# Second-layer matmuls of a unit in one run instead of small groups between first-layer products

## The chip, the cores and the metric

The kernel runs on one core of a Trainium2 chip. The time is in device microseconds (us) of one execution; three executions of the kernel before took 1178.77, 1180.59 and 1181.42 us, a median of 1180.59 us.

## The reference

Three stages follow each other. Attention over 2 x 576 tokens, 8 heads of 64, with a bias from a small network of the relative position. Then a mixture of 8 experts over the 1152 tokens, each a ReLU network 512 -> 1024 -> 512, whose outputs are weighted by a matrix P (from gate logits, normalised 8 times by rows and columns) and added. Last a network 512 -> 2048 -> 512 with ELU. All is float32.

```python
for e in range(E):                      # 8 experts
    h = np.maximum(x @ w1[e], 0.0)      # first layer
    ye = h @ w2[e]                      # second layer
    out += P[:, e:e + 1] * ye
...
h = x @ w_in                            # 512 -> 2048
g = np.where(h > 0.0, h, alpha * (np.exp(np.minimum(h, 0.0)) - 1.0))
return (g @ w_out).astype(np.float32)
```

## The kernel before

**Tiling.** The two networks are cut into 20 *halves* `he` of 512 hidden values: 0 to 15 are the halves of the 8 experts, 16 to 19 the ELU network. The tokens are two groups `n`: group 0 has 512 tokens (four tiles of 128), group 1 has 640 (five tiles). One *step* is (he, n); steps run in the order (0,0), (0,1), (1,0) and so on. The change touches 30 of the 40 steps.

**First layer.** A step has two *units* `u` of 256 hidden values. A unit is a 2 x 2 block product done with seven products in place of eight; sums of weight blocks and token blocks are prepared before. Float32 precision comes from splitting each operand into a high and a low part, so a product is 6 matmuls on TensorE (`m`, line 539): two halves of the contraction by three pairs (high-high, high-low, low-high). They are 256 columns wide in group 0 and 320 in group 1. The seven products of a unit use three PSUM banks: 1, 4, 6 and 7 add up in `b1`, 3 and 5 in `b2`, 2 is alone in `b3`. After a product ScalarE copies the bank out (`fork`, line 552, tiles `p1`, `p5`, `u2`, `u3`) or VectorE adds two parts (`add`, line 571, tiles `c1`, `c22`). A later product may add to a bank only when the copy of the earlier state is done: 6 waits for `p1`, 7 for `u2`, 3 for `p5`, and 4 for `u3`, the copy after 7. Product 4 of a unit is therefore done inside the next unit (`prev`). Then `hidden` applies ReLU or ELU and splits the result into high `hh` (ScalarE, line 602) and low `hl` (VectorE, line 605).

**Second layer.** The tokens' tiles of step (he, n) are multiplied by the second weights in the *next* step: `l2` yields 12 matmuls (`y`, line 727, 512 columns) for each token tile, four hidden blocks f by three pairs. So a step after group 0 has 48 of them and one after group 1 has 60. Tiles 0 and 1 are done together (f 0 and 1 of both, then f 2, then f 3), so that tile 0 ends with matmul 21 and tile 1 with matmul 24; the tiles behind them go one by one. In the ELU halves three tiles go together and the third has a bank of its own. Else a tile takes one of two PSUM banks (`psB`). When a tile is done, VectorE adds it to the accumulator (`l2_evac`, line 758, `acc<-y,P,acc`), and only then can the next tile but one use the bank.

**What sets the order.** `mm` gives every matmul of the two networks a rank, so TensorE's order is the order in which the code yields them: `step` runs through the products of `l1` and after product number i lets `ys`, the second-layer matmuls, advance to a share of their count:

```python
adv(lead + round((ny - lead) * max(0, i + 1 - o) / (m - o - finish)))
```

With 14 products and 48 or 60 `ys`, 3 to 5 second-layer matmuls stand behind every product. VectorE, ScalarE, GpSimd and the DMA queue of SyncE are filled by a list scheduler (`Plan.order`) with costs written into the code; each engine then runs its own list in order. `hooks` start the splitting of the next weights (`split1`) after a given product. Beside this work VectorE converts the last network's weights from float64 (`conv`, tiles `cw`, `ca`, `cb`).

Of the kernel before, what the change touches and what calls it, by code (L numbers as in the profile page):

```python
# [18 lines left out]
E = 8  # L19
# [67 lines left out]
class Plan:  # L87
# [3 lines left out]
    def buf(self, tag, bufs, alloc, tile=None):  # L91
        b = Buf(tag, alloc, tile)
        q = self.tags.setdefault(tag, [])
        b.prev = q[-bufs] if len(q) >= bufs else None
        b.before = q[-1] if q else None
        if b.prev is not None:
            b.prev.closed = True
        b.closed = False
        q.append(b)
        return b  # L100

    def op(self, eng, fn, r=(), w=(), after=(), ready=0.0, rank=None):
        o = Op()
        o.eng = eng if isinstance(eng, list) else [eng]
        o.fn, o.ready, o.idx, o.rank = fn, ready, len(self.ops), rank
        deps = set(after)
        for k in list(r) + list(w):
            b = k[0]
            assert not b.closed, b.tag
            if k in w:  # L110
                if b.prev is not None:
                    deps.update(b.prev.users)
                if b.before is not None:
                    deps.update(b.before.first)
                if not b.users or not b.first_done:
                    b.first.append(o)
            else:
                b.first_done = True
            b.users.append(o)
        for k in r:  # L120
            rd, wr = self.last.setdefault(k, ([], []))
            deps.update(wr)
        for k in w:
            rd, wr = self.last.setdefault(k, ([], []))
            deps.update(rd)
            deps.update(wr)
        for k in w:
            self.last[k] = ([], [o])
        for k in r:
            if k not in w:  # L130
                self.last[k][0].append(o)
        deps.discard(o)
        o.deps = deps
        self.ops.append(o)
        return o
# [85 lines left out]
def attention_moe_elu_ffn_kernel(  # L221
# [77 lines left out]
    def w1_sum(t, st, i, eng):  # L299
        r = t.rearrange("p (o k f) -> p o k f", o=2, k=2)  # L300
        a11, a12, a21, a22 = r[:, 0, :, 0:128], r[:, 1, :, 0:128], r[:, 0, :, 128:256], r[:, 1, :, 128:256]
        x, y, op = [
            (a21, a22, ALU.add), (st[:, 0], a11, ALU.subtract), (a11, a21, ALU.subtract), (a12, st[:, 1], ALU.subtract),
        ][i]
        eng.tensor_tensor(out=st[:, i], in0=x, in1=y, op=op)
# [70 lines left out]
    def cD(n, psum=0):  # L376
        return 0.16 + 0.00105 * n + 0.05 * psum
# [4 lines left out]
    def build():  # L382
# [44 lines left out]
        def hi_lo(b, key, dst, src, srck, n, after=(), alt=False):  # L427
            bh, bl = b

            def hi(e):  # L430
                if e == "A":
                    act.activation(out=dst(bh.get()), in_=src(), func=ACTF.Copy)  # L432
                else:
                    dve.tensor_copy(dst(bh.get()), src())

            op([("A", cA(n))], hi, r=srck, w=[(bh, key)], after=after)
            op(
                [("D", cD(n))],
                lambda e: eng[e].tensor_tensor(  # L439
                    out=dst(bl.get()), in0=src(), in1=dst(bh.get().bitcast(F32)), op=ALU.subtract  # L440
                ),
                r=srck + [(bh, key)],
                w=[(bl, key)],
                after=after,
            )

        def new_st():
            return buf("st", 1, lambda: stp.tile([128, 4, 2, 128], F32, tag="st", name="st"))

        def split1(he, u):  # L450
            if he >= HE or (he, u) in wt:
                return
            t = rawb[1, he, u]
            wt[he, u] = b = [
                buf(f"w1{x}", 2, lambda x=x: wgt.tile([128, 7, 2, 128], F32R, tag=f"w1{x}", name=f"w1{x}")) for x in "hl"
            ]
            st = new_st()
            for i in range(4):
                op(
                    [("D", cD(256))],  # L460
                    lambda e, i=i: w1_sum(t.get(), st.get(), i, eng[e]),
                    r=[(t, 0)] + ([(st, i - 1)] if i in (1, 3) else []) + ([(st, 1)] if i == 3 else []),
                    w=[(st, i)],
                )
            for i in range(4):
                n = 256 if i == 1 else 512
                dst = [slice(0, 2), 2, slice(3, 5), slice(5, 7)][i]
                hi_lo(
                    b, i, lambda x, dst=dst: x[:, dst], lambda i=i: w1_src(t.get(), st.get())[i][1],
                    [(t, 0)] if i < 2 else [(st, 2 * i - 4), (st, 2 * i - 3)], n, alt=he >= 2 * E,  # L470
                )
            load_next()
# [211 lines left out]

        prev = [None]

        def l1(he, n):
            for u in range(2):
                x = None
                for i in (1, 4, 2, 5, 6, 3, 7):  # L690
                    if i == 4:
                        if prev[0] is None:
                            continue
                        product(prev[0], 4)
                        evac(prev[0], 4)
                    else:
                        if x is None:
                            x = unit(he, n, u)
                        product(x, i)
                        evac(x, i)  # L700
                    yield i
                prev[0] = x
# [297 lines left out]
        def step(he, n, ys, ny, lead=0, finish=0, hooks={}, tail=0):  # L1000
            m = 14
            done = 0

            def adv(k):
                nonlocal done
                while done < min(k, ny):
                    next(ys)
                    done += 1

            adv(lead)  # L1010
            for i, _ in enumerate(l1(he, n)):
                o = 0 if lead or he < 2 * E or n else L2_OFF
                adv(lead + round((ny - lead) * max(0, i + 1 - o) / (m - o - finish)))
                for f in hooks.get(i, ()):
                    f()
            adv(ny)
            if not tail:
                for _ in ys:
                    pass
# [6 lines left out]
        for _ in l1(0, 0):  # L1026
            pass
# [8 lines left out]
        for he in range(HE):  # L1036
            for n in range(2):
                if (he, n) in ((0, 0), (2 * E, 1)):
                    continue
                if he == 2 * E and n == 0:  # L1040
                    for t in (0, 2, 1, 3):
                        x2t(t)
                    flush()
                    new_ops(0)
                    ops_build(0, 0)
                    ops_build(0, 1)
                    split1(he, 0)
                    ys = l2(he - 1, 1, order1)
                    step(he, 0, ys, 60 - BD_TAIL, lead=BD_LEAD, finish=BD_FIN, hooks={0: [lambda: split1(he, 1)]}, tail=1)
                    flush()  # L1050
                    for _ in ys:
                        pass
                    for t in (4, 8, 5, 7, 6):
                        x2t(t)
                    new_ops(1)
                    for t in (2, 3, 4):
                        ops_build(1, t)
                    split2(he, 0)
                    split2(he, 1)
                    step(he, 1, l2(he, 0, std[0]), 48, lead=BD_LEAD2, finish=BD_FIN2)  # L1060
                    last = (he, 1)
                    continue
                hooks = {}
                if n == 0:
                    split1(he, 0)
                    hooks[1] = [lambda he=he: split1(he, 1)]
                else:
                    if he:
                        split2(he, 0)
                        split2(he, 1)  # L1070
                od = (order1 if last[0] == 2 * E - 1 else std[1]) if last[1] else (order0 if last[0] == 2 * E - 1 else std[0])
                ys = l2(*last, od)
                fin = BD_FIN0 if (he, n) == (2 * E - 1, 1) else 0
                step(he, n, ys, 60 if last[1] else 48, finish=fin, hooks=hooks)
                last = (he, n)
                if not conved:
                    conved = True
                    conv()
# [547 lines left out]
```

## Time and profile before

| what | value |
|---|---|
| three runs | 1178.77, 1180.59, 1181.42 us |
| span of the profiled execution, first to last instruction | 1178.4 us |
| time of that execution around its span | not told apart; the fastest run is 0.4 us over the span, the median 2.2 |
| TensorE busy | 1150.9 us (98%) |
| VectorE, ScalarE busy | 910.4 us (77%), 630.5 us (54%) |
| granted TensorE clock, mean | 0.992 |

Matmuls overlap: a matmul's record of 0.28 to 0.40 us begins before the one ahead of it has ended, so what a matmul costs is the distance from its start to the next one's, not its duration. TensorE's busy time is thus not a sum of costs, and the start times in the timeline are to be used.

### The profile page before, as it was taken

To read this page: it belongs to the slowest core of one execution; us is meant where nothing else is said; L and a number is where in the kernel's file an instruction comes from. 1 tells how busy PE (TensorE), PEld (TensorE's weight loads), DVE (VectorE), ACT (ScalarE), POOL (GpSimd) and SP (SyncE) were. 2 spreads that over 40 slices of the span, in tenths; PEclk is the share of its full clock that TensorE was granted. 3 is DMA by queue.
4 is the path that set the end of the run, shared out by engine and by line. 5 is a ranking of instruction groups with operands and counts; after the bars stand their busy time and mean duration, and the time that the engine had idled before them with its cause. 6 is when DMAs were issued, how large, how long until landed. Compare 5 with 4: busy or idle time off the path is not lost.

```text
span 1178.4 us, 19626 instructions
## 1 busy us (share of the span) xinstructions
PE 1150.9 (98%) x7432; PEld 1001.2 (85%) x7432; DVE 910.4 (77%) x1936; ACT 630.5 (54%) x1428; POOL 68.0 (6%) x91
## 2 busy tenths in 40 slices
PE   7899999999999999999999999999999998999998
PEld 3467988989888898998988988989889887898987
DVE  7887888845687878878778788787776569888875
ACT  7997677644243344444443444444434347776763
POOL 0102552000000000000000000000000002000000
PEclk8999999999999999999999999999999999999999
DMA  7866631111112233333242333332411101111102
GB/s 212 252 220 213 197 112 49 37 54 55 36 40 96 65 105 91 107 92 105 66 132 68 103 91 107 94 103 70 128 46 54 44 11 51 40 54 37 36 1 81
DMA packets 36286, 104.78 MB, mean 89 GB/s; under 512 B 4065, under 2 KB 4193, under 8 KB 36193
## 3 DMA queue, kind: packets, MB, share of 16 engines
q1 hardware_dynamic: 36192, 103.54, 29.1%
q8 instruction: 58, 0.95, 0.3%
q14 instruction: 36, 0.29, 0.1%
HBM read 81.88 MB, written 21.64 MB: 88 GB/s over the span
## 4 chain that ended last, share of the span: by engine, by line
PE 90%; DVE 3%; ACT 1%; issue 1%; POOL 0%; DVEq 0%; ACTq 0%; POOLq 0%
PE y L727 41%; PE m L539 37%; PE sc L1220 3%; PE av L1302 3%; PE tr L1271 2%; PE bps L1424 1%; PE av L1312 1%; PE av L1299 1%; PE lg L883 0%; PE trl L1283 0%; DVE ol L439 0%; ACT et L1245 0%; PE x2t L977 0%; DVE w2l L439 0%; DVE et L1230 0%
## 5 line engine op out<-in xcount | busy, mean ns | idle before, releaser
L539 PE MATMUL m<-oh,w1h 128*128 128x256 f32 (+1 forms) x1120 | 331.3, 296 | 0.5 <-ACT u L552 0.5
L539 PE MATMUL m<-ol,w1h 128*128 128x256 f32 (+1 forms) x1120 | 330.7, 295 | 0.9 <-DVE ol L439 0.8
L539 PE MATMUL m<-oh,w1l 128*128 128x256 f32 (+1 forms) x1120 | 330.2, 295 | 0.0
L727 PE MATMUL y<-w2h,hh 128*128 128x512 f32 x720 | 284.2, 395 | 3.2 <-ACT hh L646 1.5
L727 PE MATMUL y<-w2l,hh 128*128 128x512 f32 x720 | 283.3, 393 | 0.8 <-DVE w2l L439 0.8
L727 PE MATMUL y<-w2h,hl 128*128 128x512 f32 x720 | 283.8, 394 | 0.0
L539 PEld LDWEIGHTS m<-ol,w1h 128*128 128x128 f32 x1120 | 211.8, 189 | 25.2 <-DVE ol L439 1.1
L539 PEld LDWEIGHTS m<-oh,w1h 128*128 128x128 f32 x1120 | 211.6, 189 | 24.7 <-ACT u L552 1.2
L539 PEld LDWEIGHTS m<-oh,w1l 128*128 128x128 f32 x1120 | 211.7, 189 | 0.1
L727 PEld LDWEIGHTS y<-w2h,hh 128*128 128x128 f32 x720 | 135.2, 188 | 19.0 <-ACT hh L646 2.3
L552 ACT ACTIVATE p<-m 128x256 f32<-128x256 f32 (+1 forms) x160 | 65.8, 411 | 158.6 <-PE m L539 154.5
L727 PEld LDWEIGHTS y<-w2h,hl 128*128 128x128 f32 x720 | 135.2, 188 | 17.6
L727 PEld LDWEIGHTS y<-w2l,hh 128*128 128x128 f32 x720 | 135.3, 188 | 16.3 <-DVE w2l L439 1.4
L552 ACT ACTIVATE u<-m 128x256 f32<-128x256 f32 (+1 forms) x160 | 65.8, 411 | 123.3 <-PE m L539 122.9
L602 ACT ACTIVATE hh<-c 128x512 fp32r<-128x512 f32 (+3 forms) x128 | 72.1, 564 | 104.0 <-DVE c L571 104.0
L758 DVE SCALAR_TENSOR_TENSOR acc<-y,P,acc 128x512 f32<-128x512 f32 x126 | 94.5, 750 | 37.9 <-PE y L727 35.7
L605 DVE SCALAR_TENSOR_TENSOR hl<-c,hh 128x512 fp32r<-128x512 f32 (+3 forms) x128 | 77.5, 606 | 20.3 <-ACT hh L602 18.4
L571 DVE TENSOR_TENSOR c<-m,u 128x256 f32<-128x256 f32 (+1 forms) x80 | 36.6, 457 | 56.7 <-PE m L539 56.1
L1230 DVE CUSTOM_DVE_ANT_0 et<-sc,bt 128x576 f32<-128x576 f32 (+1 forms) x80 | 58.0, 751 | 13.5 <-PE sc L1220 12.2
L1245 ACT ACTIVATE et<-et,nmx 128x576 f32<-128x576 f32 (+1 forms) x80 | 61.6, 775 | 0.2 <-DVE nmx L1230 0.2
L432 ACT ACTIVATE w2h<-raw 128x512 fp32r<-128x512 f32 x80 | 48.6, 626 | 21.5 <-PE y L727 11.8
L439 DVE TENSOR_TENSOR w2l<-raw,w2h 128x512 fp32r<-128x512 f32 x80 | 53.9, 692 | 1.5 <-ACT w2h L432 1.5
(138 smaller groups left out, 1550.0 us busy)
## 6 DMA issues: line engine op xcount, KB each, us to landing
raw<-w1p SPq DMA_DIRECT2D x32, 512.0 KB, 3.7
raw<-w2p SPq DMA_DIRECT2D x32, 512.0 KB, 3.6
scr<-o SPq DMA_DIRECT2D x36, 295.5 KB, 3.0
bt<-scr SPq DMA_DIRECT2D x16, 576.0 KB, 4.4
cw<-w1d SPq DMA_DIRECT2D x16, 512.0 KB, 4.6
wsc<-ca SPq DMA_DIRECT2D x32, 256.0 KB, 4.4
cw<-w2d SPq DMA_DIRECT2D x16, 512.0 KB, 4.4
raw<-wsc SPq DMA_DIRECT2D x16, 512.0 KB, 3.6
```

The costliest lines, as they stand in the source:

```text
L432: act.activation(out=dst(bh.get()), in_=src(), func=ACTF.Copy)
L439: lambda e: eng[e].tensor_tensor(out=dst(bl.get()), in0=src(), in1=dst(bh.get().bitcast(F32)), op=ALU.subtract),
L539: lambda e, w=w, o=o, j=j, k=k: pe.matmul(x["ap"](bank), w.get()[:, ai, j, :], o.get()[:, bi, j, :], start=(k == 0 and i in (1, 2, 5)), st ...
L552: lambda e: act.activation(out=b.get()[:, 0:N], in_=x["ap"](bank), func=ACTF.Copy),
L571: lambda e: eng[e].tensor_tensor(out=blk(b.get()[:, half * N:half * N + N], rev), in0=ap(p), in1=ap(q), op=ALU.add),
L602: op([("A", cA(w))], lambda e: act.activation(out=hh(), in_=ap(), func=ACTF.Relu), r=sk, w=wh, after=gate_)
L605: lambda e: dve.scalar_tensor_tensor(out=bl.get()[:, d], in0=ap(), scalar=0.0, in1=hhf(), op0=ALU.max, op1=ALU.subtract),
L727: lambda e, a=a, w=w, f=f, i=i, y=y, c=c: pe.matmul(y.get(), a.get()[:, c], w.get(), start=(f == 0 and i == 0), stop=(f == 3 and i == 2)),
L758: lambda e: dve.scalar_tensor_tensor(out=a.get(), in0=y.get(), scalar=P[0][:, n, e_:e_ + 1], in1=a.get(), op0=ALU.mult, op1=ALU.add),
L1220: pe.matmul(sc[h][0:r, x, 0:HALF], qs[:, h, qc], w[:, h, kc], start=not last, stop=last)
L1230: dve.tensor_tensor_reduce(out=e.rearrange("p (x j) -> p x j", x=2), in0=sc[0:r, :, 0:HALF], in1=biast[hp, t][0:r, h].rearrange("p (x j) - ...
L1245: act.activation(out=e, in_=e, func=ACTF.Exp, scale=-1.0, bias=nmx[0:r, h:h + 1], accum_out=sm[0:r, h:h + 1])
```

## The change

In the steps of halves 3 to 14 and 17 to 19 (`solid`) the products of a unit come in the order 1 2 4 5 6 3 7 in place of 1 4 2 5 6 3 7. No second-layer matmul stands behind products 1, 2, 4, 5, 3 and 7; behind product 6 of the first unit comes one run of half of them (24 or 30), behind product 6 of the second unit the rest. The hook that splits the next weights moves with product 4 from place 1 to place 2. The other steps are as before. Every instruction's work is unchanged.

```diff
+        def solid(he):
+            return 3 <= he < 2 * E - 1 or he > 2 * E
+
         def l1(he, n):
             for u in range(2):
                 x = None
-                for i in (1, 4, 2, 5, 6, 3, 7):
+                for i in (1, 2, 4, 5, 6, 3, 7) if solid(he) else (1, 4, 2, 5, 6, 3, 7):
...
             adv(lead)
-            for i, _ in enumerate(l1(he, n)):
+            for i, k in enumerate(l1(he, n)):
+                if solid(he) and not lead:
+                    if k == 6:
+                        adv(ny if i > 6 else (ny + 1) // 2)
+                    for f in hooks.get(i, ()):
+                        f()
+                    continue
...
                 if n == 0:
                     split1(he, 0)
-                    hooks[1] = [lambda he=he: split1(he, 1)]
+                    hooks[2 if solid(he) else 1] = [lambda he=he: split1(he, 1)]
```

The first place is on TensorE, in the first unit of step (7, 0), where the first two token tiles of the second layer end and the third begins. Before, with `y_6452` the first tile, `y_6476` the second, `y_6547` the third, and `m` a product of the first layer:

```order
L727 MATMUL y_6452<-w2h_6193,hl1_6461 128x512
L539 MATMUL m_6501<-oh0_2695,w1h_6359 128x256
L539 MATMUL m_6501<-ol0_2696,w1h_6359 128x256
L539 MATMUL m_6501<-oh0_2695,w1l_6368 128x256
L539 MATMUL m_6501<-oh0_2695,w1h_6359 128x256
L539 MATMUL m_6501<-ol0_2696,w1h_6359 128x256
L539 MATMUL m_6501<-oh0_2695,w1l_6368 128x256
L727 MATMUL y_6476<-w2h_6193,hh1_6454 128x512
L727 MATMUL y_6476<-w2l_6204,hh1_6454 128x512
L727 MATMUL y_6476<-w2h_6193,hl1_6461 128x512
L727 MATMUL y_6547<-w2h_5772,hh1_6310 128x512
```

Now at the same place (`y_6469`, `y_6483` and `y_6517` are the three tiles; the line of the matmul is 730 in the changed file):

```order
L730 MATMUL y_6469<-w2h_6162,hl1_6471 128x512
L730 MATMUL y_6483<-w2h_6162,hh1_6458 128x512
L730 MATMUL y_6483<-w2l_6169,hh1_6458 128x512
L730 MATMUL y_6483<-w2h_6162,hl1_6471 128x512
L730 MATMUL y_6517<-w2h_5777,hh1_6302 128x512
```

The product that stood between the end of the first tile and the start of the third has moved away; three matmuls are left between them.

The second place is on VectorE, in the same unit: the additions of these two tiles to the accumulators `acc4` and `acc5`, and what stands ahead and behind. Before:

```order
L439 TENSOR_TENSOR w1l_6480<-raw_6077,w1h_6473 128x256
L834 TENSOR_SCALAR cb_6465<-ca_6348 128x512
L837 SCALAR_TENSOR_TENSOR cb_6465<-cw_6297,cb_6465 128x512
L842 TENSOR_TENSOR ca_6348<-ca_6348,cb_6465 128x512
L758 SCALAR_TENSOR_TENSOR acc4_3516<-y_6452,P_4096,acc4_3516 128x512
L571 TENSOR_TENSOR c1_6495<-m_6501,u2_6528 128x256
L758 SCALAR_TENSOR_TENSOR acc5_3533<-y_6476,P_4096,acc5_3533 128x512
```

Now:

```order
L439 TENSOR_TENSOR w1l_6461<-st_6389,w1h_6450 128x512
L439 TENSOR_TENSOR w1l_6461<-raw_6055,w1h_6450 128x256
L840 SCALAR_TENSOR_TENSOR cb_6370<-cw_6205,cb_6370 128x512
L845 TENSOR_TENSOR ca_6279<-ca_6279,cb_6370 128x512
L761 SCALAR_TENSOR_TENSOR acc4_3516<-y_6469,P_4096,acc4_3516 128x512
L761 SCALAR_TENSOR_TENSOR acc5_3533<-y_6483,P_4096,acc5_3533 128x512
L571 TENSOR_TENSOR c1_6446<-m_6448,u2_6474 128x256
```

The two additions now follow each other; a piece of the weight conversion (`cb`, `ca`) still stands right ahead of them.

## Rows read from the trace of the kernel before

**Rows 1.** The page's chain that ended last, by line.

```profile
PE y L727 41%; PE m L539 37%; PE sc L1220 3%; PE av L1302 3%; PE tr L1271 2%; PE bps L1424 1%; PE av L1312 1%; PE av L1299 1%; PE lg L883 0%; PE trl L1283 0%; DVE ol L439 0%; ACT et L1245 0%; PE x2t L977 0%; DVE w2l L439 0%; DVE et L1230 0%
```

**Rows 2.** Windows: stretch, length, busy us and count by engine, granted clock, DMA.

```profile
358.00:910.00 552.00, 552.00 (x3234) 497.02 (x3233) 433.18 (x814) 234.87 (x499) 0.00 (x0) 1.00 0.30 91
1060.00:1110.00 50.00, 50.00 (x294) 45.06 (x294) 42.62 (x85) 34.09 (x75) 2.46 (x2) 1.00 0.14 43
```

**Rows 3.** Timeline (start, us, instruction): first matmul of steps (7,0), (7,1), (8,0).

```profile
532.99 0.28 PE L539 MATMUL m<-oh,w1h 128*128 128x256 f32 x1
...
556.90 0.30 PE L539 MATMUL m<-oh,w1h 128*128 128x320 f32 x1
...
580.09 0.28 PE L539 MATMUL m<-oh,w1h 128*128 128x256 f32 x1
```

**Rows 4.** Timeline of the last 60 second-layer matmuls: number 1, 7 and 51.

```profile
1160.06 0.39 PE L727 MATMUL y<-w2h,hh 128*128 128x512 f32 x1
...
1161.44 0.39 PE L727 MATMUL y<-w2h,hh 128*128 128x512 f32 x1
...
1171.41 0.39 PE L727 MATMUL y<-w2h,hl 128*128 128x512 f32 x1
```

**Rows 5.** Timeline of first-layer matmuls in long runs: 24 of 256, 25 of 320.

```profile
212.67 0.28 PE L539 MATMUL m<-oh,w1h 128*128 128x256 f32 x1
...
215.38 0.28 PE L539 MATMUL m<-oh,w1l 128*128 128x256 f32 x1
...
953.24 0.31 PE L539 MATMUL m<-oh,w1l 128*128 128x320 f32 x1
...
956.76 0.31 PE L539 MATMUL m<-oh,w1l 128*128 128x320 f32 x1
```

**Rows 6.** Timeline, a wait for a bank: VectorE's addition, the two matmuls behind.

```profile
332.87 0.75 DVE L758 SCALAR_TENSOR_TENSOR acc<-y,P,acc 128x512 f32<-128x512 f32 x1
...
333.68 0.50 PE L727 MATMUL y<-w2h,hh 128*128 128x512 f32 x1 [0.33 <-DVE acc L758]
...
334.01 0.40 PE L727 MATMUL y<-w2l,hh 128*128 128x512 f32 x1
```

**Rows 7.** Waits: all of TensorE's waits for such an addition.

```profile
PE y L727 <- DVE acc L758: 1.0, 2, 0.7
```

**Rows 8.** Timeline of step (7,0): VectorE ahead of the addition, and TensorE.

```profile
539.90 0.69 DVE L837 SCALAR_TENSOR_TENSOR cb<-cw,cb 128x512 f32<-128x512 uint32 x1
...
541.31 0.40 PE L727 MATMUL y<-w2h,hl 128*128 128x512 f32 x1
...
541.74 0.75 DVE L758 SCALAR_TENSOR_TENSOR acc<-y,P,acc 128x512 f32<-128x512 f32 x1 [0.42 <-PE y L727]
...
542.93 0.40 PE L727 MATMUL y<-w2h,hh 128*128 128x512 f32 x1
```

**Rows 9.** Lines by form: ScalarE's weight split and bank copy (count, busy, mean ns).

```profile
L432 ACT ACTIVATE w1h<-st 128x512 fp32r<-128x512 f32 x76 | 44.5, 622 | 2.0 <-DVE st L305 1.9
...
L552 ACT ACTIVATE u<-m 128x256 f32<-128x256 f32 x80 | 30.7, 384 | 60.5 <-PE m L539 60.2
```

**Rows 10.** Timeline at step (17,0): end of product 1, start of product 4.

```profile
1017.79 0.28 PE L539 MATMUL m<-oh,w1l 128*128 128x256 f32 x1
...
1018.23 0.42 PE L539 MATMUL m<-oh,w1h 128*128 128x320 f32 x1 [0.16 <-ACT u L552]
...
1018.48 0.31 PE L539 MATMUL m<-ol,w1h 128*128 128x320 f32 x1
```

**Rows 11.** Timeline: first matmul of steps (18,0), (18,1), (19,0).

```profile
1064.77 0.28 PE L539 MATMUL m<-oh,w1h 128*128 128x256 f32 x1
...
1088.72 0.31 PE L539 MATMUL m<-oh,w1h 128*128 128x320 f32 x1
...
1111.92 0.28 PE L539 MATMUL m<-oh,w1h 128*128 128x256 f32 x1
```

**Rows 12.** Windows: a stretch with several waits of TensorE (columns as in rows 2).

```profile
996.50:1003.00 6.50, 4.97 (x19) 4.33 (x20) 6.26 (x16) 2.48 (x6) 1.74 (x3) 0.74 0.29 83
```

## The prediction

> **What bounds the kernel now.** I read the chain of waits first: 78% of the span is matmuls of the two layers [rows 1]. The windows of the changed stretch come next: from 358 to 910 us, nearly all of halves 3 to 14, TensorE is busy 552.00 of 552.00 us at the full one of its two clock levels, and VectorE, the next engine, 433 us [rows 2]. So no time can be won there by removing waits: there are none. Only the distances between matmuls can shrink, and any new wait is paid in full. The timeline gives the distances. A pair of steps takes 556.90 - 532.99 = 23.91 us and 580.09 - 556.90 = 23.19 us [rows 3], 12 times nearly alike.
>
> What would the same matmuls cost in long runs? The last 60 second-layer matmuls have no product between them: from the 7th to the 51st they take 9.97 us, 0.2266 us each; the six distances before the 7th take 1.38 us, 0.02 more than 6 x 0.2266 [rows 4]. First-layer matmuls in long runs take 2.71 / 23 = 0.1178 us (256 columns) and 3.52 / 24 = 0.1467 us (320) [rows 5]. A step of group 0 holds 60 second-layer matmuls, 78 of 256 and, in the product 4 that it inherits, 6 of 320: 13.60 + 9.19 + 0.88 = 23.67 us, where 23.91 was measured. A step of group 1 holds 48, 78 of 320 and 6 of 256: 10.88 + 11.44 + 0.71 = 23.03, where 23.19 was measured. So 14 small groups cost 0.24 and 0.16 us a step over long runs. I take this as the price of the beginning of a group, some 12 to 17 ns each.
>
> **The change part by part.**
>
> *Fewer groups.* Per step 14 groups become 2, and each run pays its beginning once, about 0.025 us. Steps of group 0 gain 0.24 - 0.05 = 0.19 us, of group 1 0.16 - 0.05 = 0.11: 0.30 a half, 3.6 us for halves 3 to 14. In the ELU halves the steps take 23.95 and 23.20 us [rows 11], 0.28 and 0.17 over the sum; less 0.05 each that is 0.35 a half, 1.05 for three. Together **-4.7 us**. Bounds: nothing, if the distance does not come from the grouping; -6.2 (12 x 0.40 + 3 x 0.45), if a run's beginning cost nothing.
>
> This row speaks against a rule of the Trainium skill, page "TensorE: Matmul & The Clock Gate", section "Back-to-back issue gap": the gap between matmuls follows from their column count alone, with a small constant. The trace disagrees: 512 columns cost 0.2266 us in a long run and more in short groups. By that rule this term would be 0; that is a rival below.
>
> *A new wait for a bank.* In the 12 steps of group 0 in halves 3 to 14 the first run is 30 matmuls. Tile 0 ends with matmul 21, and matmul 25 begins tile 2 in the same bank. Before, four matmuls and a product lay between their starts, 542.93 - 541.31 = 1.62 us [rows 8]. Now there are four distances, 0.91 us. The bank needs: start of matmul 21 to start of the addition 541.74 - 541.31 = 0.43, the addition 0.75 [rows 8], its end to the waiting matmul 333.68 - 333.62 = 0.06 [rows 6]: 1.24 us. TensorE therefore waits 0.33 us, if VectorE is free. The wait does not end cleanly: after the one in rows 6 the next distance is 334.01 - 333.68 = 0.33 in place of 0.23, 0.10 more, and I add 0.03 for the slow beginning. That is 0.46 us a place, 12 places, **+5.5 us**. Such waits are nearly absent before: two in the whole trace, 1.0 us [rows 7]. Queued behind the waiting matmul on TensorE are the rest of the run and products 3 and 7; nobody else is late for them, since the other engines wait for TensorE.
>
> Is VectorE free there? Before, it had been idle for 0.42 us when the tile ended [rows 8]. Matmul 21 again has the same five products and 20 matmuls in front of it, so the addition is asked for at the same time, about 8.3 + 0.4 us after the step's start. The products come earlier than before. What comes later is the split of the next weights, which ScalarE now does behind the copy after product 6: that product ends about 3.9 us into the step (four products of 0.71, one of 0.88), the copy takes 0.38, three splits 3 x 0.62 [rows 9], so 6.2; then VectorE has one low part and the two conversion pieces of up to 0.69 each [rows 8], about 8.2. So some 0.4 us of margin stay. Bounds: 0.33 + 0.13 when free, and 0.69 more for a whole such instruction in the way. I take free, nearest to the idle row.
>
> The runs of 24 end exactly with tile 1, so their third tile comes a whole stretch later: no wait. In the second runs of 30, 12 matmuls (2.7 us) lie between a bank's last use and its next: no wait.
>
> *ELU steps of group 1.* Three tiles go together, and in the second run of 24 matmul 13 takes the bank that matmul 6 ended: seven distances, 1.59 us against 1.24. VectorE is busy 42.6 of 50 us there [rows 2], so one instruction in the way can cost up to its length less 0.35. Three places, 0 to 0.4 us each: **+0.5**.
>
> *Product 4 after 2.* It waits for the copy `u3` after product 7, with two products between (1.4 us or more), where a product and two groups of second-layer matmuls stood before (2.1 us or more). The matmul's record runs 0.28 us on and the copy takes 0.38 [rows 3, 9]: hidden with 0.7 us to spare, 0. At the beginning of step (17,0) no second-layer matmul stood there, and product 4 began 0.44 us after the last matmul of product 1 in place of 0.12, with the next distance 0.10 too long [rows 10]. Now product 2 covers it: **-0.4**. If another ScalarE instruction takes the cover's place, 0.
>
> Sum: -4.7 + 5.5 + 0.5 - 0.4 = **+0.9 us** on the span of 1178.4, 1179.3. The median of the runs stands 2.2 us over this span; with the same offset the forecast is **1181.5 us**. The work of every engine stays the same; the weights' loads and their splits keep whole steps of room.
>
> **The rivals.**
>
> *The wait for the bank does not come* (VectorE's addition is through in time, or the bank is not what the matmul waits for). For: the trace of before has almost none. Against: the chain of 1.24 us is made of three measured pieces, and the order shows the third tile three matmuls behind the first. Then -5.5 falls out of the sum: 1176.0 us, faster.
>
> *Distance depends on the width alone* (the skill's rule above), so regrouping wins nothing. For: the conversion and split work that runs beside the small groups is absent at the end of the kernel, so the short distances there may have another cause. Against: the first six distances of that last run are longer than the rest with the same work beside them. Then +4.7: 1186.2 us, slower.
>
> *VectorE is late at the bank.* The place is the conversion piece right ahead of the addition, in 12 steps; it decides once VectorE comes more than 0.4 us later than worked out. One instruction of 0.69 too late then costs 0.3 more at 12 places, +3.5: 1185.0 us, slower.
>
> *The clock falls.* In one stretch TensorE waited 1.5 of 6.5 us and its granted clock was 0.74 [rows 12], so part of it ran at 1.2 GHz. If the wait of each run did that, as in that stretch 0.26 x 6.5 = 1.7 us a place would be lost, +20 us: 1202 us. Against: the waits come once in 47 us and are a fifth as long. The page named above, section "A second HAM failure mode: psum-queue depth-cycling", tells of a clock that oscillates when banks are cycled; no row here shows it for single waits.
>
> **How the numbers follow.** Chances: forecast 0.62, no bank wait 0.10, width alone 0.10, VectorE late 0.14, clock 0.02, the rest 0.02. What a measurement can tell from no change is 0.2%, 2.4 us. The forecast's own range is 1179 to 1184: within 2.4 us in most of its chance, above it in about a tenth. So faster 0.12, same 0.57, slower 0.31. The range of 8 in 10 reaches to the rivals on the slow side and most of the way to the fast one: 1178.0 to 1187.0 us.
>
> **What would show it.** In the profile after, steps of group 0 in halves 3 to 14 should take about 23.91 - 0.19 + 0.46 = 24.2 us, of group 1 23.1 us; TensorE should wait 12 times about 0.33 us at the second layer for an addition to an accumulator; the distances from the seventh matmul of a run on should be 0.227 us. Steps of group 0 below 23.8 us would prove the bank term wrong, above 24.5 us VectorE's margin; distances of 0.231 deep in a run the first term. Waits of the first layer for a ScalarE copy would show a mistake about product 4.

## The result and the profile after

The changed kernel takes 1194.9 us (median of 4 runs, 1192.4 to 1195.1) beside 1179.7 us for the kernel before: ratio 1.0121, 95% interval 1.0103 to 1.0138. It is 15 us slower where +0.9 was forecast, and lies above the range. The profiled execution has a span of 1193.0 us against 1178.4. In the whole document lines up to L684 are the same in both kernels; L727, L758, L814 to L845 of before are L730, L761, L817 to L848 after.

The changed steps themselves came out nearly as forecast. The timeline of TensorE, first matmul of steps (7,0), (7,1) and (8,0), answers to [rows 3]:

```profile
534.22 0.28 PE L539 MATMUL m<-oh,w1h 128*128 128x256 f32 x1
...
558.30 0.32 PE L539 MATMUL m<-oh,w1h 128*128 128x320 f32 x1
...
581.38 0.28 PE L539 MATMUL m<-oh,w1h 128*128 128x256 f32 x1
```

A step of group 0 takes 24.09 us (before 23.91), one of group 1 23.08 (before 23.19): +0.18 and -0.11. The next lines are the end of tile 0 in step (7,0), VectorE's addition and TensorE's two matmuls behind it (start, us, instruction, idle time and releaser); they answer to [rows 6, 8]:

```profile
542.80 1.43 DVE L761 SCALAR_TENSOR_TENSOR acc<-y,P,acc 128x512 f32<-128x512 f32 x2 [0.43 <-PE y L730]
...
543.05 0.39 PE L730 MATMUL y<-w2h,hl 128*128 128x512 f32 x1
...
543.61 0.50 PE L730 MATMUL y<-w2h,hh 128*128 128x512 f32 x1 [0.17 <-DVE acc L761]
...
543.95 0.40 PE L730 MATMUL y<-w2l,hh 128*128 128x512 f32 x1
```

From 543.05 to 543.61 is 0.56 us where a long run has 0.23, so the wait adds 0.33; the next distance of 0.34 is 0.11 too long. Both are the sizes of the forecast. The waits of TensorE for that addition, whole trace, against [rows 7] (total, times, longest):

```profile
PE y L730 <- DVE acc L761: 4.3, 14, 2.0
```

Twelve of the 14 are these, and one of 0.3 us is that of [rows 6]; the last, of 2.0 us, is new, and it leads to the loss. Adding up the two traces by steps: ahead of (3,0) +0.85, halves 3 to 14 +0.90, (15,1) **+5.4**, (16,0) **+9.3**, (16,1) -2.5, (17,0) to (19,0) -0.8, the end behind them +1.4. The change does not touch the code of halves 15 and 16. What differs there? The windows give it (columns as in [rows 2]). First the kernel before, steps (15,1) and (16,0):

```profile
933.70:968.27 34.57, 33.23 (x186) 29.18 (x184) 20.21 (x39) 15.89 (x33) 0.74 (x1) 1.00 0.10 31
968.27:996.13 27.86, 26.39 (x164) 22.65 (x162) 26.16 (x52) 20.52 (x46) 4.25 (x5) 1.00 0.13 38
```

The kernel after, halves 3 to 14 but for the first step, then (15,1) and (16,0):

```profile
359.70:911.50 551.80, 549.98 (x3226) 495.25 (x3225) 407.10 (x767) 221.99 (x491) 0.00 (x0) 1.00 0.25 79
...
935.43:975.37 39.94, 34.83 (x186) 30.03 (x185) 34.47 (x62) 17.69 (x37) 3.09 (x3) 0.94 0.30 93
975.37:1012.57 37.20, 30.77 (x163) 24.96 (x162) 33.45 (x69) 21.98 (x47) 2.67 (x3) 0.91 0.23 71
```

VectorE, the third pair of numbers, does 407 us in 767 instructions where it did 433 in 814 [rows 2]: it has **less** to do in the changed halves. Most of the 26 us turn up here: 34.5 us in place of 20.2 in (15,1), 33.5 in place of 26.2 in (16,0). Whose work is it? The conversion's: 32 items that turn the last network's float64 weights into float32, which no engine waits for until half 15, and which the planner's list puts into VectorE's free time. Each ends with a store `wsc<-ca`. The stores by line, over the whole kernel and in step pair (8,0), (8,1) (count, shortest/median/longest in ns, first and last start), of before:

```profile
L845 SPq DMA_DIRECT2D wsc<-ca x32: 326/326/953, 372.4 to 871.0; - x32
L845 SPq DMA_DIRECT2D wsc<-ca x3: 326/326/326, 588.4 to 612.4; - x3
```

and of after: over the whole kernel, and from the start of (15,1) to the end of (16,0):

```profile
L848 SPq DMA_DIRECT2D wsc<-ca x32: 319/326/327, 370.2 to 992.3; - x32
...
L848 SPq DMA_DIRECT2D wsc<-ca x6: 319/320/320, 941.0 to 992.3; - x6
```

Before, three items a half, the last at 871.0 us. After, two a half (589.6 and 609.6 in half 8), the last at 992.3 us. Six fall into (15,1) and (16,0), where VectorE also moves x2t, builds the operands and later runs the ELU.

In (15,1) TensorE waits for VectorE (total, times, longest):

```profile
PE y L730 <- DVE hl L605: 3.0, 1, 3.0
PE y L730 <- DVE acc L761: 2.0, 1, 2.0
```

and the chain of waits shows what stands ahead of `hl` and `acc` in VectorE's list (start, us, what):

```profile
964.97 0.75 DVE ca L820
...
965.74 0.44 DVE cb L827
...
966.21 0.70 DVE ca L832
...
966.93 0.43 DVE cb L837
967.36 1.20 DVE ol L439 x2
...
969.08 1.03 DVE hl L605
970.11 0.88 DVE st L338
970.99 0.60 DVE ca L845
971.59 0.33 DVE st L338
971.92 0.67 DVE acc L761
```

`ca` and `cb` are the conversion: about 3 us of it on the path. In (16,0) TensorE waits above all for the ELU's result `hh` and for `w1l`, a split of weights on VectorE:

```profile
PE y L730 <- ACT hh L646: 2.5, 2, 1.6
PE m L539 <- DVE w1l L439: 2.3, 2, 1.9
```

There the chain runs through two whole items, one after the other:

```profile
981.87 0.60 DVE ca L845
...
982.49 5.20 DMA wsc<-ca
987.74 0.04 issue
987.78 0.68 ACT ca L817
988.48 0.70 DVE ca L820
...
991.58 0.69 DVE ca L845
992.28 0.61 DVE w1l L439
...
992.93 3.19 PE m L539 x22
...
996.21 0.38 ACT u L552
996.59 0.53 ACT a L630
```

There is one buffer `ca`, so the last item waits 5.2 us for the store of the one before. The split `w1l` of the next weights stands behind that item in VectorE's list, and 22 matmuls and a copy stand behind the split. Only then comes the ELU's first operation (L630), at 996.5. Before, it came 20 us earlier:

```profile
L630 ACT ACTIVATE a<-c x2: 401/512/623, 976.8 to 980.3; 128x512 f32<-128x512 f32 x1, 128x256 f32<-128x256 f32 x1
```

The program has a second reason for a late ELU: its tiles take over the conversion's memory (`swap`, `cv_end`), so the planner puts L630 behind the last store in the lists, and it may not run before that store has landed, here at 994.7 us. I call this the gate. Two candidates, then, besides late weight loads, for how a late conversion costs time: VectorE's work, and the gate.

### The profile page after: what moved, and what is told of

Its sections match the earlier page's. It is cut to its first block, busy times and chain, and to the rows that moved or that the text cites. A ratio compares the mean times of both kernels' runs of the same rounds, so it can differ in the third digit from the quotient of the medians.

```text
span 1193.0 us, 19677 instructions
## 1 busy us (share of the span) xinstructions
PE 1156.0 (97%) x7432; PEld 1002.0 (84%) x7432; DVE 907.8 (76%) x1930; ACT 622.9 (52%) x1428; POOL 73.0 (6%) x97
## 4 chain that ended last, share of the span: by engine, by line
PE 86%; DVE 6%; ACT 2%; issue 1%; POOL 0%; DMA 0%; DVEq 0%; ACTq 0%; POOLq 0%
PE y L730 39%; PE m L539 36%; PE sc L1229 3%; PE av L1311 3%; PE tr L1280 2%; PE bps L1433 1%; DVE acc L761 1%; PE av L1321 1%; PE av L1308 1%; PE lg L886 0%; DMA wsc<-ca 0%; PE trl L1292 0%; DVE a L639 0%; DVE hl L649 0%; DVE hl L605 0%
## 5 line engine op out<-in xcount | busy, mean ns | idle before, releaser
L730 PE MATMUL y<-w2h,hh 128*128 128x512 f32 x720 | 285.6, 397 | 8.1 <-DVE acc L761 4.3
L730 PE MATMUL y<-w2h,hl 128*128 128x512 f32 x720 | 283.5, 394 | 4.0 <-DVE hl L605 3.0
L730 PE MATMUL y<-w2l,hh 128*128 128x512 f32 x720 | 283.1, 393 | 0.0
L730 PEld LDWEIGHTS y<-w2h,hh 128*128 128x128 f32 x720 | 135.9, 189 | 39.3 <-DVE acc L761 9.9
L730 PEld LDWEIGHTS y<-w2h,hl 128*128 128x128 f32 x720 | 136.2, 189 | 32.3 <-DVE hl L605 3.4
L730 PEld LDWEIGHTS y<-w2l,hh 128*128 128x128 f32 x720 | 136.1, 189 | 23.2
L761 DVE SCALAR_TENSOR_TENSOR acc<-y,P,acc 128x512 f32<-128x512 f32 x126 | 92.8, 750 | 66.2 <-PE y L730 65.9
```

The costliest lines, as they stand in the source:

```text
L730: lambda e, a=a, w=w, f=f, i=i, y=y, c=c: pe.matmul(y.get(), a.get()[:, c], w.get(), start=(f == 0 and i == 0), stop=(f == 3 and i == 2)),
L761: lambda e: dve.scalar_tensor_tensor(out=a.get(), in0=y.get(), scalar=P[0][:, n, e_:e_ + 1], in1=a.get(), op0=ALU.mult, op1=ALU.add),
```

## The experiments

Theory 1 is that the conversion's place decides and the grouping itself moves little. The table has every run: the start of the last store, the three steps at the boundary, and the ratio to the kernel before on the same chip.

| run | last store, us | (15,1) | (16,0) | (16,1) | ratio (95%) |
|---|---|---|---|---|---|
| before | 871.0 | 34.57 | 27.86 | 21.07 | 1 |
| after | 992.3 | 39.94 | 37.21 | 18.59 | 1.0121 (1.0103-1.0138) |
| e1 solid 17 to 19 | 871.7 | 34.56 | 27.87 | 19.54 | 1.0012 (0.9996-1.0027) |
| e2 solid 3 to 14 | 991.6 | 39.93 | 36.76 | 18.28 | 1.0120 (1.0099-1.0141) |
| e3 old, light items | 650.4 | 34.56 | 27.88 | 19.52 | 1.0011 (0.9998-1.0023) |
| e4 new, light items | 665.2 | 34.56 | 27.87 | 20.83 | 1.0010 (0.9997-1.0023) |
| e5 e4 with runs 24, 36 | 601.3 | 34.56 | 27.87 | 20.84 | 0.9969 (0.9953-0.9984) |
| e6 new, runs 24, 36 | 955.2 | 34.56 | 27.87 | 19.52 | 0.9967 (0.9954-0.9981) |
| e7 new, two `ca` | 939.9 | 34.56 | 27.87 | 19.52 | 1.0011 (1.0000-1.0022) |
| e8 e6 and e7 together | 852.3 | 34.56 | 27.87 | 20.86 | 0.9971 (0.9960-0.9983) |
| e9 old, late by 70 us | 939.5 | 34.55 | 27.87 | 21.06 | 1.0003 (0.9989-1.0016) |
| e10 old, late by 115 us | 985.5 | 35.40 | 37.06 | 18.05 | 1.0070 (1.0050-1.0089) |
| e11 new, other loads | 992.5 | 39.93 | 37.76 | 18.12 | 1.0117 (1.0098-1.0135) |
| e12 product order only | 979.2 | 34.55 | 30.28 | 18.77 | 1.0020 (1.0006-1.0033) |
| e13 old, last item late | 993.7 | 34.56 | 43.30 | 16.04 | 1.0094 (1.0077-1.0111) |
| e14 the same, later | 1001.6 | 34.57 | 48.80 | 16.03 | 1.0157 (1.0139-1.0175) |
| e15 old, light items, late | 983.6 | 34.46 | 35.85 | 16.04 | 1.0035 (1.0022-1.0048) |

One warning on (16,1). The kernels in which it takes 19.5 us and those in which it takes 20.8 to 21.1 have the same waits there (1.5, 0.8 and 0.8 us), but the granted clock was 1.00 in the first and 0.92 in the second; the kernel before is one of the second. By the steps, the price of the boundary is therefore counted from 47.4 us for (16,0) and (16,1) together, as in e1, e3, e6 and e7. Why the clock differed is not shown.

**e1 and e2: where the loss comes from.** The condition of `solid(he)` was cut in two: `he > 2 * E`, and `3 <= he < 2 * E - 1`.

> Runs of y only in halves 17 to 19; halves 3 to 14 in the old order. Theory 1 (in halves 3 to 14 the weight conversion gets through two items a half instead of three, and what is left of it falls into halves 15 and 16, where VectorE is needed for x2t and the operands; the grouping by itself moves little): the conversion's last store stays at about 871 us as before, the part from (15,1) to (16,1) takes 83.5 us as before, and the total is 1179.4 us (1177.5 to 1181.5; by the two traces halves 17 to 19 together moved by less than 1 us). Rival A (it is the new order of halves 17 to 19 that shifts the deadlines of the lists and so the boundary at 15 and 16): 1192 to 1196 us.

> Runs of y only in halves 3 to 14; halves 17 to 19 in the old order. Theory 1: the whole loss is here, 1195 us (1192.5 to 1197), with (15,1) to (16,1) at 95 us or more and the last store of the conversion near 992 us. Rival A: 1180 to 1182 us.

e1 took 1181.0 us, e2 1192.4 us. The whole loss comes with halves 3 to 14, though it is paid in 15 and 16; rival A falls.

**e3 and e4: the conversion made light.** In both kernels:

```
-  op([("D", 0.42)], ... tensor_scalar(I(b), I(a), 3, 0x3FFFFFF8, ...
-  op([("D", 0.69)], ... M_SE ...
-  op([("D", 0.42)], ... M_EXP ...
-  op([("D", 0.81)], ... in0=wl(), scalar=2.0 ** -52 ...
-  op([("D", 0.74)], ... tensor_tensor(out=a.get(), in0=a.get(), in1=b.get() ...
```

> The kernel before, with five of the seven arithmetic operations of each conversion item left out (the last four halves then work on other weights). Theory 1: the conversion stands on no path in the kernel before, so the time stays: 1179.7 us (1177.5 to 1182). Rival B (VectorE's load as such sets the pace): 1170 us or less.

> The changed kernel with the same five operations of each conversion item left out. Theory 1: the conversion is done long before half 15, the 14 us are gone, and what is left is the grouping itself: e3 + 0.9 us, 1180.6 us (1178 to 1183.5). Rival C (the boundary is late for another reason than the conversion: the lists' deadlines, the clock): the loss stays, e3 + 12 to 15 us.

1179.7 and 1180.6 us: 0.9 apart, the figure of the forecast's sum for the grouping. That agreement is luck: both intervals are some 3 us wide, and by the steps the two differ by +0.55 us in halves 3 to 14, -1.1 in (17,0) to (19,0), +1.4 at the end and +1.3 in (16,1), where the clocks differ. With the conversion out of the way the change costs nothing that these runs can tell. Rivals B and C fall.

**e5 and e6: the wait for the bank taken away.** The first run ends with tile 1, so that no tile begins behind it in the same run:

```
-                        adv(ny if i > 6 else (ny + 1) // 2)
+                        adv(ny if i > 6 else 24)
```

> As e4 (five operations of each conversion item left out), and the 60 matmuls of y of a step with n=0 go in runs of 24 and 36 instead of 30 and 30, so that the first run ends with the second tile and no tile begins right behind it in the same run. The price of the wait for the bank: if the two stalls of 0.32 and 0.11 us in each of the 12 steps are that wait and nothing else, a step with n=0 falls from 24.09 to about 23.65 us and the total by 12 x 0.44 = 5.3 us, to e4 - 5.3 = 1175.3 us (1173.5 to 1177.5). Rival D (the wait only moves to the second run, at its third tile): no change against e4.

> The changed kernel with the whole conversion, runs of 24 and 36. The bank wait is gone (-5.3 us), and VectorE's list has other holes: if the conversion gets through more than two items a half, it ends earlier than 992 us and less of it falls into halves 15 and 16. Theory 1: the time follows the conversion's last store: near 992 us 1189 us, near 955 us 1180 us, near 871 us 1175 us. Rival C: 1189 us whatever the last store.

e5 took 1175.9 us. A step of group 0 fell from 24.09 to 23.63 us, 0.46 less (in the last two of the 12 halves 0.27, since e4 had 23.90 there), and TensorE has no wait at all in halves 3 to 14 where e4 still had these:

```profile
PE y L730 <- DVE acc L761: 2.0, 12, 0.2
```

(the view counts 0.17 us of each; the distances say 0.46). Rival D falls. e6, with the whole conversion, took 1175.7 us, as fast as e5 and below the 1180 expected for a last store near 955 us. The store does come at 955.2, and the boundary is that of before. The windows of e6, (15,1) and (16,0):

```profile
931.52:966.08 34.56, 33.22 (x185) 29.18 (x184) 27.00 (x52) 16.21 (x34) 0.74 (x1) 1.00 0.21 61
966.08:993.95 27.87, 26.40 (x164) 22.67 (x162) 26.16 (x52) 20.52 (x46) 4.24 (x5) 1.00 0.13 38
```

VectorE has 27.0 us to do in (15,1), 7 more than before and 7 less than after, and that fits for nothing. So the cost does not grow with each us of delay; it begins somewhere behind 955 us, 11 us ahead of the start of (16,0). e6 is 3.8 us faster than the kernel before.

**e7 and e8: a second buffer for `ca`.** In `conv()` and for the tile's other user, `logits()`:

```
-  buf("cv" + c, 1, ... pools["cv"].tile(s, d, tag=c, ...))
+  buf("cv" + c, 2 if c == "a" else 1, ... pools["cv"].tile(s, d, tag=c, ..., bufs=2 if c == "a" else 1))
```

> The changed kernel with two buffers for the conversion's tile ca instead of one, so that an item begins while the one before is still being stored; nothing else. Theory 1: the conversion gets through more items in each half and ends earlier than 992 us, and the boundary (15,1) to (16,1) comes down with it: 1182 us (1180 to 1189). Rival E (VectorE has no room at all in these halves for a third item, whatever the buffers): 1195 us.

> Both: two buffers for ca and runs of 24 and 36. Theory 1: the conversion is done before half 15, the boundary is as before, the bank wait is gone: before + 0.9 - 5.3 = 1175 us (1173 to 1178), faster than both kernels. Rival C or E: 1185 us or more.

1180.7 and 1175.5 us. With the grouping left exactly as in the changed kernel, 2 KB of memory a partition take 14 us back; rival E falls. e8 equals e6: once the conversion is early enough, earlier is worth nothing.

**e9 and e10: the loss without any grouping.** In the kernel before, only `CV_T0 = 40.0` became 240.0 and 300.0 (the planner's time from which an item may begin).

> The kernel before, its order of products and of y untouched; only the conversion may begin later, by six items, so that its last store comes at about 941 us instead of 871. Theory 1: the place of the conversion decides, not the grouping; a last store at 940 to 955 us was free in e6 and e7, so before + 0: 1179.5 us (1177.5 to 1182). Rival F (it needs the grouped steps for the loss): also 1179.5.

> The same with the conversion later still, its last store between 975 and 995 us as in the changed kernel. Theory 1: a loss without any grouping, 5 to 14 us, 1185 to 1194 us. Rival F: 1179.5 us.

1180.0 and 1187.8 us. The old order pays 8 us once its conversion ends at 985.5 us; rival F falls. In (16,0) and (16,1) it takes 55.1 us, nearly the 55.8 of the changed kernel; only (15,1) stays cheaper, with three stores in it instead of four.

**e11: the weights that load late.** The loads of the last four halves read other rows, every list the same:

```
-  sp.dma_start(out=b.get(), in_=raw_src(*it))
+  sp.dma_start(out=b.get(), in_=raw_src(it[0], it[1] % (2 * E), it[2]))
```

> The changed kernel, every engine's list the same, but the weight loads of the last four halves read other rows of memory, which the conversion doesn't write (so the last four halves work on other weights): no load waits for a store of the conversion. Theory 1a (the 14 us are VectorE's time: eight items of the conversion, about 4 us each, stand in its list between the operands' pieces): unchanged, 1194 us (1190 to 1196). Theory 1b (the 14 us are weights that come late, since their loads wait for the last stores): before + 1 to 4 us, 1180 to 1184.

1193.7 us: unchanged. So 1b falls. It does not prove 1a, as the expectation put it: the ELU's gate was still there.

**e12: the product order alone.** The branch `if solid(he) and not lead:` in `step` became `if False:`.

> Only the other half of the change: product order 1 2 4 5 6 3 7 in halves 3 to 14 and 17 to 19, y spread between the products as before, no runs. Theory 1: as in every kernel here the conversion's last store tells: if it comes by 955 us the total is within 3 us of before, if near 980 to 990 us it is 5 to 12 us slower. Of the grouping's own terms none applies.

1181.6 us, with the last store at 979.2. The expectation had 5 to 12 us for a store "near 980"; it cost about 2, and the steps show where: (16,0) takes 2.4 us more, of which (16,1) gives some back. So the cost begins between 955 and 979 us and is 8 us by 985.5. The order alone delays the conversion by 108 us, the runs of y by 13 more; the runs in the old order were not tried. The steps of halves 3 to 14 take 23.91 and 23.21 us in e12: the order by itself moves them by no more than 0.02 us.

**e13 to e15: VectorE's time or the ELU's gate.** In e13 and e14 the kernel before holds back one item:

```
-  after=attn_end, ready=CV_T0,
+  after=attn_end, ready=780.0 if len(wscw) == 31 else CV_T0,
```

(795.0 in e14); e15 is e3 with `CV_T0 = 490.0`.

> The kernel before with 31 of the 32 conversion items at their old times, so that VectorE has none of their work in halves 15 and 16; only the last item may not begin before a given moment, and its store comes near 992 us. Theory 1g (at (16,0) the price is the gate: the ELU's first operation waits for the last store, since its tiles take the conversion's memory; it came 4.2 us behind the last store in the changed kernel, 996.5 after 992.3, and is wanted at 976.8 in the kernel before; by e12, e10 and the changed kernel the step pays what exceeds about 5.7 us of that lateness): ELU at about 997, 20 us late, before + 14 us, 1194 us (1189 to 1198), all of it in (16,0) and (16,1), none in (15,1). Theory 1v (the price is VectorE's time for six to eight items): one item, before + 0 to 2 us, 1180 to 1182.

> The same with the last store some 14 us later, near 1007 us. Theory 1g: as much more again, e13 + 14 us, 1208 us (1202 to 1213). Theory 1v: e13 + 0.

> e3 (five of the seven operations of each item left out) with the conversion begun so late that its last store comes near 985.5 us, as in e10, which was 8 us slower than the kernel before. Theory 1g: the store's place decides, whatever VectorE did for it: before + 6 to 8 us, 1187 us (1184.5 to 1189). Theory 1v: a third of the work, before + 1 to 3 us, 1182 us.

1190.7, 1197.3 and 1183.7 us. In e13 VectorE has one item more at the boundary, (15,1) costs nothing, and (16,0) takes 43.3 us. Its ELU begins, by line, and TensorE waits in that step for the ELU's result:

```profile
L630 ACT ACTIVATE a<-c x1: 612/612/612, 997.6 to 997.6; 128x512 f32<-128x512 f32 x1
```

```profile
PE y L727 <- ACT hh L646: 13.0, 1, 13.0
```

So the gate alone can cost 11 us: 1v is wrong as the whole cause. 1g is right in kind and too dear in size: e14's store came 7.9 us later than e13's instead of 14, and 6.6 us were added instead of 14. e14 is also the one run in which ScalarE stands idle until the store has landed (timeline, idle and releaser):

```profile
1004.06 0.63 ACT L630 ACTIVATE a<-c 128x512 f32<-128x512 f32 x1 [8.14 <-DMA wsc<-ca]
```

In the changed kernel, e10, e13 and e15 the store had landed 1.6 to 2.2 us before L630 began; those last 2 us are its place behind other work in ScalarE's list.

In e15 the last store stands 17.7 us behind the start of (16,0), much as in e10 and the changed kernel (17.0 and 16.9; 26.6 in e13), with a fifth of VectorE's work in each item (one instruction of 0.70 us left of six, 3.7 us): (16,0) and (16,1) take 4.5 us more than in e3, where e10 has 7.7 more by the same count, and 0.8 in (15,1). Both ways count. For the changed kernel, set against e7 which has the same grouping: (15,1) +5.4 us, where the gate cannot act and e13 shows nothing, is VectorE's work (e15 has four light items there too, and (15,1) costs nothing); of the +8.4 in (16,0) and (16,1) about 4.5 is the gate by e15, and the rest, some 4 us, VectorE's list. That last split is an estimate across two kernels, not a measurement of its own: the chain above names VectorE's list and not the store ahead of L630.

## Why the prediction was wrong, point by point

**The step that failed** is the sentence under the sum: "The work of every engine stays the same; the weights' loads and their splits keep whole steps of room." The amount stays; its place does not. The sum followed the instructions that the change touches and the loads and splits, and left out the list's filler, the conversion, which the planner places wherever VectorE's list is free at the right moment. One of its instructions stood in the argument, the `cb` ahead of the addition [rows 8], but only as something that could be in the way; I never asked where such instructions go when they no longer fit. The order of VectorE's list would have shown two items a half in place of three. This costs 13 to 14 us by steps (15,1) to (16,1), after against e7 and e2 against e1; by the medians 14 and 11.

**Fewer groups, -4.7.** Right in kind, too small: with no wait, and with a product order that by itself changes these steps by no more than 0.02 us (e12), e5 against e3 shows 23.91 to 23.63 us in group 0, -0.28 where -0.19 was worked out, and -0.11 in group 1, as worked out. Over 12 halves that is 4.7 us in place of 3.6. The rival "distance depends on the width alone" is wrong: the same matmuls, with no wait in either list, take 0.28 us a step less in two runs than in 14 groups. The Trainium skill, page "TensorE: Matmul & The Clock Gate", section "Back-to-back issue gap", gives a gap by the column count alone, which it calls that of an isolated matmul, and for a stream of weight loads and matmuls one figure per column count. The prediction took the first for the rule of a stream; neither tells what grouping costs.

**The wait for a bank, +5.5.** Right: 0.46 us a place, from e6 against the changed kernel, 12 places. VectorE was free enough at the bank (0.43 idle ahead of the addition); that rival and "no bank wait" fell. So halves 3 to 14 cost +0.9 us as a whole against +1.9 forecast, the gain of the runs being larger.

**ELU halves and product 4, together -0.95.** Wrong by 1.5 us. The steps from (17,0) to (19,0) did gain 0.8 us, but the end lost 1.4. More than half of that is a place that the step on product 4 missed. The last product 4 stands right behind product 7, with no next product to cover the copy; before, matmuls of y covered it (timeline, idle and releaser):

```profile
1173.05 0.41 PE L539 MATMUL m<-oh,w1h 128*128 128x320 f32 x1 [0.80 <-ACT u L552]
```

e1 has the same 1.4 us at its end, and is +1.8 us by its median with an interval that includes none.

**The clock.** The single waits of 0.33 us did not lower it: the granted clock is 1.00 over halves 3 to 14. It fell to 0.94 and 0.91 where the long waits of (15,1) and (16,0) are. That is part of their price and hardly a cause of its own: e2, the changed kernel and e11 take 39.93 to 39.94 us in (15,1) at a granted clock of 0.96, 0.94 and 0.92.

The chance of "slower" was given 0.31 for the wrong reasons: all slow rivals sat at the bank or in the clock, none at the boundary.

## What to carry to other kernels

- When a change reorders an engine that others follow, look at the lists of the others for filler work as well, count how much of it gets through per stage before and after, and ask what waits for its end. Work without a due time moves quietly until it meets one.
- A stage in which the bounding engine is nearly 100% busy can look unharmed and still export its cost: here the changed halves lost 0.9 us and the unchanged ones 12. Compare busy times of the **other** engines by stage, in both traces.
- Put the end of a run of matmuls where a bank's tile ends: 24 and 36 instead of 30 and 30 was worth 5 us (e7 to e8), and made the grouping 3.8 us faster than the kernel before.

## What the runs showed of the hardware

- A wait of TensorE for a bank costs more than the idle time that the view of waits gives: 0.17 us there, 0.33 by the distance of the starts, 0.46 us a step with the slower distances behind it (24.09 against 23.63 us). In two of the 12 halves of e4 and four of e2 the step took 23.90 us with the same wait, so the part behind it varies; what sets it is not shown.
- With the same waits of TensorE, step (16,1) took 19.52 us in e7 at a granted clock of 1.00 and 20.84 us in e4 at 0.92.
- The part ahead of half 3, which e1, e2, e6, e11, e13 and e14 do not edit, ended between 343.5 (e13) and 347.0 us (e6) in the profiled executions. Single spans can't be compared below some 3 us; steps agree to 0.01 us (23.628 us in nearly all of e5, e6 and e8).
